# Gathering softmax row sums across partitions: one tile per parity, the first 32 partitions' sums left in place, three transfers in place of four

## The chip, the cores and the metric

The kernel runs on one core of a Trainium2 chip. The metric is device time in microseconds (us), the median of several runs. Beside the timed runs stands one profiled execution, from which every duration below is read.

## The reference, cut to what matters

Batch 8, 12 heads, 448 positions, head width 64. Attention comes first, with a soft cap on the scores, then a channel mix (RWKV style) over the 768 columns that the heads make together.

```python
scores = cap * tanh((q @ k.T) / sqrt(64) / cap)
attn = exp(scores - max);  attn = attn / (sum(attn, -1) + 1e-9)
x = attn @ v                                  # 8 x 448 x 768
xk, xr = mu_k * x + (1 - mu_k) * x_prev, mu_r * x + (1 - mu_r) * x_prev
v = relu(xk @ w_k) ** 2 @ w_v
out = sigmoid(xr @ w_r) * v
```

## The kernel before

Two heads make a pair, and 48 pairs are worked through in steps, one pair a step, followed by a few steps that only drain. The order of the work in a step is written out by hand as a string of operation names (`ROWS`, `ODD_6`, `LAST` and others), and each engine and each DMA queue executes its part of that string in order. After the steps (from about 529 us on) TensorE does the two large products with `w_v` and `w_r` and nothing else.

In a step for pair i, TensorE computes transposed scores in four groups of keys (`scores`), ScalarE applies tanh and exp, and VectorE sums the exponentials over keys. A score tile has keys on partitions, so this sum is split: `red` (line 347) transposes blocks of 32x32 and adds, which leaves on each of the four groups of 32 partitions one partial sum for every query. The sums of a pair stand in a tile `r1` of 128 partitions x 98 columns; there are two such tiles, for even and for odd i (shown in the trace as `r`).

What follows is a chain over two steps. In the string of step i+1, `gather` (line 353) issues four transfers on SP's queue, each of which moves one group of 32 partitions into a slot of `sq`, a tile of 32 partitions with eight slots, of which there is one for all pairs. `recip` (lines 357 to 364) adds the slots on VectorE, takes the reciprocal and transposes it. `rec_store` (line 367) writes it to memory from SP's queue, and `rec_load` (line 376) reads it back on SP's queue as a broadcast, two transfers into `r`. In step i+2 `norm` (line 380) multiplies the attention result in PSUM (`pv`) by it, `mix_old` (ScalarE) and `mix_new` (line 395, tile `xk`) blend it with the previous position, and that frees the PSUM bank for a later `pv`. From `xk` come the operands `xkh` and `xkl` of the product with `w_k` (line 472 and 496).

SP's queue carries nearly all other transfers too, in this order within a step of the middle of the kernel: `gather`, `weight_store` (w_d, line 614), `load_v` (rv, line 208), a weight load (line 544), `x_store` (line 424), `rec_store`, stores of k (line 521), `load_qk` (rqk, line 204) and `rec_load`. In the first six steps `rec_load` and `load_v` stand behind `gather`. Every transfer is bound to one of eight completion semaphores in turn, and is not issued before the transfer eight places ahead of it has completed.

Of the kernel before, what the change touches and what calls it, by code (L numbers as in the profile page):

```python
# [10 lines left out]
F32 = mybir.dt.float32  # L11
# [18 lines left out]
P = 128  # L30
# [17 lines left out]
NB = 2 * S // 32  # L48
RM = 3 * NB
RC = RM + NB // 2  # L50
# [57 lines left out]
class Body:  # L108
# [54 lines left out]
    def guard(self):  # L163
        nc = self.nc
        if self.maxima:
            nc.vector.memset(self.grd, 1e-9)
        else:
            nc.scalar.activation(self.grd, self.cap_t, AF.Abs)
            nc.scalar.activation(self.grd, self.grd, AF.Exp, scale=-1.0)
            nc.vector.tensor_scalar(self.grd, self.grd, 1e-9, None, op0=ALU.mult)  # L170
        nc.gpsimd.tensor_copy(self.sq[:, 6:8, RM:RC], self.grd[0:32].unsqueeze(2).to_broadcast([32, 2, NB // 2]))


    def init_x(self, pool):
# [6 lines left out]
    def init_sums(self, pool):  # L181


        nc = self.nc
        self.r1, self.sr = [], []
        self.sq = pool.tile([32, 8, RC], F32, name="sq_")
        for j in range(2):
            self.r1.append(pool.tile([P, RC], F32, name=f"r1_{j}"))
            self.sr.append(pool.tile([32, 32], F32, name=f"sr_{j}"))
            nc.gpsimd.memset(self.sr[j], 1.0)  # L190

# [157 lines left out]
                                     axis=mybir.AxisListType.X, op=ALU.add, apply_transpose=True)  # L349

    def gather(self, i):
        for q in range(4):
            self.nc.sync.dma_start(self.sq[:, q % 2 * 2 + q // 2], self.r1[i % 2][32 * q:32 * q + 32])  # L353

    def recip(self, i):
        nc, t, sq = self.nc, self.sr[i % 2], self.sq
        nc.vector.tensor_reduce(out=sq[:, 4:6, RM:RC], in_=sq[:, 0:4, 0:RM].rearrange("l q (h b g) -> l h b q g", h=2, g=3),
                                axis=mybir.AxisListType.XY, op=ALU.add)
        nc.vector.tensor_reduce(out=t[:, 0:NB].rearrange("l (h b) -> l h b", h=2),
                                in_=sq[:, :, RM:RC].rearrange("l (s h) b -> l h b s", h=2),  # L360
                                axis=mybir.AxisListType.X, op=ALU.add)
        nc.vector.reciprocal(t[:, 0:NB], t[:, 0:NB])
        self.rs[i] = self.up.tile([32, 32], F32, name="rs")
        nc.vector.transpose(out=self.rs[i], in_=t)
# [714 lines left out]
```

## Time and profile before

| | us |
|---|---|
| three timed runs | 899.71, 900.53, 900.52; median 900.52 |
| profiled execution, its own time | 896.04 |
| its span, from the first to the last instruction | 894.2 |
| TensorE busy | 860.9 (96%) |
| VectorE busy | 734.1 (82%) |

The profiled execution lies 4.48 us under the median, and 1.84 us of its time lie around its span. TensorE (PE in the profile, PEld its weight loads) is busy nearly throughout; the share says nothing yet on single stretches. DVE is VectorE, ACT ScalarE, POOL GpSimd, SPq SP's queue.

### The profile page before, as it was taken

The numbers are of one execution on the slowest core, as the hardware profiler recorded it, in microseconds if no ns is written. First come the engines' busy times: TensorE is split into PE (matmuls) and PEld (weight loads), VectorE is DVE, ScalarE is ACT, GpSimd is POOL, SyncE is SP. The second block draws the span as 40 slices with busy tenths as digits, with TensorE's granted clock in tenths as the row PEclk, the third lists the DMA queues.
The fourth block names the chain that finished last, engine by engine and source line by source line (L and its number), as shares of the span: only waits on it lengthen the run. The fifth ranks groups of instructions, "written<-read, shape, count | busy, mean of one in ns | idle before, by whom it ended". The sixth has DMA issues, their size and how long they took to land.

```text
span 894.2 us, 16687 instructions
## 1 busy us (share of the span) xinstructions
PE 860.9 (96%) x5826; PEld 705.7 (79%) x5826; DVE 734.1 (82%) x1246; ACT 625.2 (70%) x922; POOL 410.6 (46%) x345
## 2 busy tenths in 40 slices
PE   6789999999999999999999999999999999999996
PEld 2236667776766777777766799999999999999996
DVE  6989996999989989998978766887887757777775
ACT  8898888878888888788786564656565535555553
POOL 4996684777877867766853200000000033333330
PEclk9999999999999999999999999999999999999998
DMA  5565746566767667666665547554545546676763
GB/s 161 163 203 171 249 148 200 177 202 211 235 200 219 199 190 231 211 207 197 183 204 169 199 146 232 193 161 153 174 152 170 164 153 195 213 219 218 217 217 106
DMA packets 123679, 170.15 MB, mean 190 GB/s; under 512 B 22592, under 2 KB 107712, under 8 KB 123584
## 3 DMA queue, kind: packets, MB, share of 16 engines
q1 hardware_dynamic: 120848, 164.65, 59.0%
q10 hardware_dynamic: 2736, 4.33, 1.3%
q8 instruction: 48, 0.79, 0.4%
q14 instruction: 47, 0.39, 0.2%
HBM read 109.91 MB, written 56.60 MB: 186 GB/s over the span
## 4 chain that ended last, share of the span: by engine, by line
PE 72%; DVE 9%; DMA 6%; ACT 6%; POOL 3%; SPq 3%; issue 2%; ACTq 0%; DVEq 0%; POOLq 0%
PE ps L709 40%; PE kps L496 13%; PE pv L312 8%; PE s L275 5%; PE kps L472 3%; DVE r L347 3%; ACT p L288 2%; ACT p L301 2%; SPq L353 2%; DMA sq__195<-r 2%; PE pv L338 2%; PE s L268 1%; DMA rec_d<-rs 1%; DMA rv<-v 1%; DMA rqk<-qk 1%
## 5 line engine op out<-in xcount | busy, mean ns | idle before, releaser
L347 DVE TRANSPOSE_TENSOR_REDUCE r<-p 128x28 f32<-128x896 f32 (+1 forms) x192 | 181.1, 971 | 13.4 <-ACT p L301 13.4
L288 ACT ACTIVATE p<-s,scl_t 128x896 f32<-128x896 f32 x168 | 165.6, 998 | 26.8 <-PE s L268 22.5
L301 ACT ACTIVATE p<-p,cap_t 128x896 f32<-128x896 f32 x168 | 175.1, 1042 | 4.3 <-ACT ko L508 0.4
L673 POOL TENSOR_TENSOR s<-src 128x384 f32<-128x384 f32 x14 | 14.3, 1021 | 262.7 <-DVE lo L694 262.7
L312 PE MATMUL pv<-p,rv 128*64 128x448 f32 x576 | 119.8, 554 | 12.1 <-DVE xk L395 10.9
L709 PE MATMUL ps<-wvh,hi 128*128 128x384 f32 x392 | 131.1, 334 | 0.0
L709 PE MATMUL ps<-wvl,hi 128*128 128x384 f32 x392 | 131.0, 334 | 0.0
L693 ACT CAST hi<-s 128x512 fp32r<-128x512 f32 (+1 forms) x112 | 63.5, 567 | 89.6 <-PE ps L709 76.0
L694 DVE TENSOR_TENSOR lo<-s,hi 128x512 fp32r<-128x512 f32 (+1 forms) x112 | 70.8, 632 | 58.5 <-ACT hi L693 43.8
L132 POOL TENSOR_TENSOR qkl<-rqk,qkh 128x896 fp32r<-128x896 f32 x47 | 109.2, 2324 | 8.3 <-ACT qkh L126 4.8
L496 PE MATMUL kps<-xkh,wkh 64*128 64x448 f32 (+1 forms) x540 | 109.6, 367 | 0.0
L496 PE MATMUL kps<-xkl,wkh 64*128 64x448 f32 (+1 forms) x540 | 108.7, 362 | 0.0
L496 PE MATMUL kps<-xkh,wkl 64*128 64x448 f32 (+1 forms) x540 | 108.6, 361 | 0.0
L709 PE MATMUL ps<-wrh,hi 128*128 128x384 f32 x294 | 98.9, 336 | 0.3 <-DVE o L732 0.3
L709 PE MATMUL ps<-wrl,hi 128*128 128x384 f32 x294 | 98.8, 336 | 0.0
L312 PEld LDWEIGHTS pv<-p,rv 128*64 128x64 f32 x576 | 38.2, 138 | 76.5 <-issue 48.9
L693 ACT CAST hi<-src 128x512 fp32r<-128x512 f32 (+1 forms) x84 | 47.7, 568 | 62.0 <-PE ps L709 56.3
L709 PE MATMUL ps<-wvh,lo 128*128 128x384 f32 x392 | 83.7, 334 | 0.0
L694 DVE TENSOR_TENSOR lo<-src,hi 128x512 fp32r<-128x512 f32 (+1 forms) x84 | 57.3, 682 | 21.3 <-ACT hi L693 19.5
L709 PEld LDWEIGHTS ps<-wvh,hi 128*128 128x128 f32 x392 | 73.6, 188 | 0.3 <-issue 0.2
L709 PEld LDWEIGHTS ps<-wvl,hi 128*128 128x128 f32 x392 | 73.6, 188 | 0.0
L591 POOL TENSOR_TENSOR wsq<-wa,wsq 128x384 f32<-128x384 f32 (+1 forms) x40 | 43.9, 1096 | 62.9 <-DVE wsq L584 55.4
(118 smaller groups left out, 1915.0 us busy)
## 6 DMA issues: line engine op xcount, KB each, us to landing
rqk<-qk SPq DMA_DIRECT2D x47, 448.0 KB
src<-k_d SPq DMA_DIRECT2D x56, 256.0 KB
rv<-v SPq DMA_DIRECT2D x48, 256.0 KB
r<-rec_d SPq DMA_DIRECT2D x96, 112.0 KB
v_d<-o SPq DMA_DIRECT2D x56, 192.0 KB
src<-x_d SPq DMA_DIRECT2D x42, 256.0 KB
vl<-v_d SPq DMA_DIRECT2D x56, 192.0 KB
out<-o SPq DMA_DIRECT2D x55, 192.0 KB
```

Source lines behind the costliest of these rows:

```text
L132: {"p": self.nc.gpsimd, "v": self.nc.vector}[e].tensor_sub(*a)
L275: nc.tensor.matmul(s[:, (h + i) % 2, 0:S], qk[a][p, k], qk[b][p, 0:S], start=(n == 0), stop=(n == 2))
L288: self.nc.scalar.activation(p32[:, n], self.S.pop((i, g))[:, n, 0:S], AF.Tanh, scale=self.scl_t)
L301: self.nc.scalar.activation(p32, p32, AF.Exp, scale=1.0 if self.maxima else self.cap_t)
L312: nc.tensor.matmul(pv[p, 0:S], v[:, g, h, :], ph[:, (h + i) % 2, :], start=(g == 0), stop=False)
L347: self.nc.vector.tensor_reduce(out=r1[:, 0:RM].rearrange("p (x g) -> p x g", g=3)[:, :, g] if g < 3 else r1[:, RM:RC], in_=p32.rearrange(" ...
L472: nc.tensor.matmul(self.kps[fc][:, 0:S], w, m[:, dc, :], start=first, stop=last)
L496: self.nc.tensor.matmul(self.kps[c][:, 0:S], w[p, dc, c * P:(c + 1) * P], m[p, dc, :], start=s == 0, stop=last or way == 2 and t == 2, ski ...
L591: {"p": self.nc.gpsimd, "v": self.nc.vector}[e].tensor_add(sq, f(a), sq)
L693: self.nc.scalar.copy(hi, x)
L694: self.nc.vector.tensor_sub(lo, x, f(hi))
L709: self.nc.tensor.matmul(o, a[:, c, :], w[:, c, :], start=first and k == 0, stop=last and k == len(todo) - 1, skip_group_check=True)
```

## The change

The two tiles `r1` and the one tile `sq` become two tiles of 128 partitions x 8 slots x 98 columns, one for each parity. Slot 0 takes the partial sums of all 128 partitions, so those of the first 32 partitions are already where `sq` wants them. `gather` issues transfers for the other three groups only, out of slot 0 of the tile into slots 2, 1 and 3 of the same tile. `recip` reads the tile of its parity. The small constant in slots 6 and 7 is written once for each of the two tiles.

```diff
-        nc.gpsimd.tensor_copy(self.sq[:, 6:8, RM:RC], self.grd[0:32].unsqueeze(2).to_broadcast([32, 2, NB // 2]))
+        for sq in self.sq:
+            nc.gpsimd.tensor_copy(sq[:, 6:8, RM:RC], self.grd[0:32].unsqueeze(2).to_broadcast([32, 2, NB // 2]))
...
-        self.r1, self.sr = [], []
-        self.sq = pool.tile([32, 8, RC], F32, name="sq_")
+        self.r1, self.sr, self.sq = [], [], []
         for j in range(2):
-            self.r1.append(pool.tile([P, RC], F32, name=f"r1_{j}"))
+            t = pool.tile([P, 8, RC], F32, name=f"sq_{j}")
+            self.r1.append(t[:, 0])
+            self.sq.append(t[0:32])
...
     def gather(self, i):
-        for q in range(4):
-            self.nc.sync.dma_start(self.sq[:, q % 2 * 2 + q // 2], self.r1[i % 2][32 * q:32 * q + 32])
+        for q in range(1, 4):
+            self.nc.sync.dma_start(self.sq[i % 2][:, q % 2 * 2 + q // 2], self.r1[i % 2][32 * q:32 * q + 32])
 
     def recip(self, i):
-        nc, t, sq = self.nc, self.sr[i % 2], self.sq
+        nc, t, sq = self.nc, self.sr[i % 2], self.sq[i % 2]
```

Line numbers behind line 171 grow by up to two. On SP's queue the order of the other transfers stays, but with one transfer fewer in each step the semaphores are dealt out differently. Here is SP in a step of the middle (the one whose rv load is issued at 343 us), before; a name in `waits` that begins with DMAHW is one of the eight completion semaphores, and a transfer without such a wait is one whose semaphore was waited for already:

```order
L204 DMA rqk<-qk 128x896 [waits DMAHW0_49,PE_49]
L376 DMA r<-rec_d_97 64x448 [waits DMAHW5_49,DMAHW1_49]
L376 DMA r<-rec_d_97 64x448 [waits DMAHW2_49]
L353 DMA sq__195<-r_0_196 32x98 [waits DMAHW3_49,DVE_49]
L353 DMA sq__195<-r_0_196 32x98 [waits DMAHW4_49]
L353 DMA sq__195<-r_0_196 32x98
L353 DMA sq__195<-r_0_196 32x98 [waits DMAHW6_49]
L614 DMA w_d<-wsq 128x384 [waits DMAHW7_49,Pool_49]
L208 DMA rv<-v 128x512 [waits DMAHW0_49]
L544 DMA w_4387<-wv 128x768 [waits DMAHW1_49]
```

And the same step with the change:

```order
L206 DMA rqk<-qk 128x896 [waits DMAHW0_49,PE_49]
L378 DMA r<-rec_d_97 64x448 [waits DMAHW5_49,DMAHW1_49]
L378 DMA r<-rec_d_97 64x448 [waits DMAHW2_49]
L355 DMA sq_195<-sq_195 32x98 [waits DMAHW3_49,DVE_49]
L355 DMA sq_195<-sq_195 32x98 [waits DMAHW4_49]
L355 DMA sq_195<-sq_195 32x98
L616 DMA w_d<-wsq 128x384 [waits DMAHW6_49,Pool_49]
L210 DMA rv<-v 128x512 [waits DMAHW7_49]
L546 DMA w_4354<-wv 128x768 [waits DMAHW0_49]
```

One of the four transfers of 32x98 is gone; the transfer that waits for semaphore 0, on which the rqk load of the same step completes, was the rv load and is now the weight load behind it.

On VectorE nothing moves. Around the `recip` of pair 46, near the end of the steps, VectorE's rows are these before:

```order
L380 TENSOR_TENSOR x_163<-pv,r 128x448 [waits DMAHW7_49,DMAHW0_49,PE_49]
L357 TENSOR_REDUCE sq__195<-sq__195 32x2x14 [waits DMAHW3_49,DMAHW4_49,DMAHW2_49,DMAHW1_49]
L359 TENSOR_REDUCE sr_197<-sq__195 32x28 [waits DVE_49]
L362 RECIPROCAL sr_197<-sr_197 32x28 [waits DVE_49]
L364 STREAM_TRANSPOSE rs<-sr_197 32x32 [waits DVE_49]
L395 SCALAR_TENSOR_TENSOR xk<-x_163,mu_k,pv 128x448 [waits Activation_49]
```

and these with the change:

```order
L382 TENSOR_TENSOR x_163<-pv,r 128x448 [waits DMAHW2_49,DMAHW1_49,PE_49]
L359 TENSOR_REDUCE sq_195<-sq_195 32x2x14 [waits DMAHW4_49,DMAHW5_49,DMAHW3_49,DVE_49]
L361 TENSOR_REDUCE sr_196<-sq_195 32x28 [waits DVE_49]
L364 RECIPROCAL sr_196<-sr_196 32x28 [waits DVE_49]
L366 STREAM_TRANSPOSE rs<-sr_196 32x32 [waits DVE_49]
L397 SCALAR_TENSOR_TENSOR xk<-x_163,mu_k,pv 128x448 [waits Activation_49]
```

The first reduction waits for three transfers and for VectorE's own earlier sums, where it waited for four transfers.

## Rows read from the trace of the kernel before

**Rows 1.** The page, part 1: busy us, share of the span, instructions.

```profile
PE 860.9 (96%) x5826; PEld 705.7 (79%) x5826; DVE 734.1 (82%) x1246; ACT 625.2 (70%) x922; POOL 410.6 (46%) x345
```

**Rows 2.** Windows of 50 us: busy us of each engine, granted clock, DMA share, GB/s.

```profile
0.00:50.00 50.00, 34.67 (x192) 14.25 (x194) 38.68 (x74) 42.98 (x51) 36.36 (x39) 0.96 0.57 175
...
450.00:500.00 50.00, 47.84 (x354) 33.49 (x351) 39.37 (x55) 31.21 (x39) 21.43 (x18) 1.00 0.51 167
```

**Rows 3.** Waits of PE, 0 to 131 us: total us, times, longest.

```profile
PE pv L312 <- DVE xk L395: 9.3, 7, 3.0
```

**Rows 4.** Waits of PE, 131 to 440 us.

```profile
PE s L275 <- ACT turned L503: 1.3, 4, 0.3
PE pv L312 <- DMA rv<-v: 1.3, 3, 0.5
```

**Rows 5.** Waits of PE, 440 to 530 us.

```profile
PE kps L472 <- ACT ko L508: 1.6, 2, 1.1
PE pv L312 <- DVE xk L395: 1.6, 1, 1.6
```

**Rows 6.** Tile sq: engine, duration in ns (min/median/max), first and last start.

```profile
L353 SPq DMA_DIRECT2D sq__195<-r x192: 517/582/1572, 15.0 to 495.7; - x192
...
L171 POOL COPY sq__195<-grd x1: 197/197/197, 10.6 to 10.6; 32x28 f32<-32x28 f32 x1
```

**Rows 7.** Timeline of SP's queue, 338 to 345 us: start, us, line.

```profile
339.50 2.93 SPq L353 DMA_DIRECT2D sq__195<-r  x4
...
343.10 0.43 SPq L208 DMA_DIRECT2D rv<-v  x1
```

**Rows 8.** Chain of waits, 340 to 346 us: start, us, what.

```profile
343.10 3.77 DMA rv<-v
```

**Rows 9.** Chain of waits, 440 to 470 us: one round of the sums.

```profile
453.56 0.54 SPq L353
...
455.41 1.79 DMA sq__195<-r
...
458.81 3.71 DMA rec_d<-rs
...
463.76 0.54 SPq L353
```

**Rows 10.** Chain of waits, 485 to 503 us.

```profile
487.30 1.79 DMA sq__195<-r
...
490.67 0.56 DVE xk L395
...
495.67 3.17 DMA sq__195<-r
...
500.25 0.61 DVE x L380
```

**Rows 11.** Waits of DVE, whole span: total us, times, longest.

```profile
DVE sq__195 L357 <- DMA sq__195<-r: 14.0, 19, 1.9
```

**Rows 12.** Waits of SP's queue, whole span.

```profile
SPq L376 <- DMA rec_d<-rs: 69.6, 42, 5.0
```

**Rows 13.** Timeline of POOL, 5 to 36 us; in brackets idle time before.

```profile
18.15 1.01 POOL L591 TENSOR_TENSOR wsq<-wa,wsq 128x384 f32<-128x384 f32 x1 [4.30 <-DVE wsq L584]
...
35.06 1.00 POOL L591 TENSOR_TENSOR wsq<-wa,wsq 128x384 f32<-128x384 f32 x1 [0.25 <-DVE wsq L584]
```

**Rows 14.** Timeline of SP's queue, 10 to 64 us.

```profile
22.05 0.36 SPq L204 DMA_DIRECT2D rqk<-qk  x1
22.52 2.42 SPq L353 DMA_DIRECT2D sq__195<-r  x4
```

**Rows 15.** Timeline of DVE, 10 to 64 us.

```profile
27.83 0.51 DVE L357 TENSOR_REDUCE sq__195<-sq__195 32x28 f32<-32x336 f32 x1 [1.00 <-DMA sq__195<-r]
```

**Rows 16.** Timeline of DVE, 500 to 535 us: the last operands prepared for w_v.

```profile
516.16 3.56 DVE L835 TENSOR_TENSOR wvl<-wvl,wvh 128x768 fp32r<-128x768 f32 x4
```

**Rows 17.** Tile wvh, 500 to 560 us: the first weight load of the last stage.

```profile
L709 PEld LDWEIGHTS ps<-wvh,hi x60: 187/188/188, 529.1 to 559.3; 128*128 128x128 f32 x60
```

## The prediction

> **What bounds the kernel now.** The page's first part comes first: TensorE is busy for 860.9 of 894.2 us [rows 1], so no change to transfers can be worth more than some 33 us, and the question is where those lie. The windows of 50 us tell [rows 2]. In the first, TensorE is busy for only 34.67 us; at the end of the steps it is idle for 2.16 us in 50. Behind 529 us it does nothing but matmuls, and what those need is ready early: the last operand for `w_v` is made at 516.16 + 3.56 = 519.7 us and the first weight load of that stage starts at 529.1 [rows 16, 17]. So whatever brings TensorE earlier to the end of the steps comes off the end of the span, as long as it stays under that lead of 9 us.
>
> Next I asked what TensorE waits for, stage by stage. Up to 131 us its largest wait is for `xk`, 9.3 us [rows 3]; from there to 440 us it waits for 2.6 us in all, half of that for the load of rv [rows 4]; from 440 us to the end of the steps it waits for 3.2 us, for a PSUM bank freed by `xk` and for k sums taken over by ScalarE [rows 5]. A gain must come out of these three sums. The chain of waits then shows why the transfers of the sums matter at all: near the end of the steps it runs round and round through them [rows 9, 10].
>
> **What the change removes.** One issue on SP's queue in each of 48 steps. An issue takes 0.58 us in the median [rows 6]; four took 2.42 us and 2.93 us at the two places shown [rows 7, 14], and from the first issue at 453.56 to the last at 455.41 are 1.85 us, three spacings of 0.62 [rows 9]. After the last issue begins, the data are there 1.79 us later [rows 9, 10]. I take **0.61 us**: the last group starts so much earlier, and everything behind it on SP (w_d, rv, the weight load, `x_store`) too.
>
> The semaphores may help as well: in the step shown the rv load stands eight places behind the rqk load of 448 KB and waits for it, and with the change the weight load stands there. TensorE shows no rv wait longer than 0.5 us [rows 4], which the 0.61 cover already, so I add nothing for it. Behind the weight load on SP stand `x_store` and `rec_store`; it reaches that wait at the very time at which rv reached it before, so they lose nothing either.
>
> **What it adds.** One more copy of 0.20 us on POOL at 10.6 us [rows 6]; POOL then stands idle for 4.30 us before its work at 18.15 [rows 13], which covers it; uncovered it would cost 0.2 us once. The reduction on VectorE now also waits for VectorE's own earlier sums. The transfers for which it waits read those same sums, so the sums are always done first: nothing. The sums, the reductions and the reciprocal keep their shapes.
>
> **First stage, 0 to 131 us.** Here VectorE, ScalarE and POOL share the limit. At 27.83 the reduction waited 1.00 us for the gather [rows 15], but right ahead of that gather stands an rqk load of 448 KB [rows 14]: the last of the four issues ended at 24.94 and the data landed 2.9 us later, where 1.79 less the issue, 1.2 us, is usual. The landing may thus be that of rqk. What follows is caught by POOL, which waited for VectorE only 0.25 us at 35.06 [rows 13]. Term: 0.2 us; bounds 0 and 0.6 (one issue, if the landing counts in full).
>
> **Middle, 131 to 440 us.** Three times TensorE stands still for rv, together 1.3 us, none longer than 0.5 us [rows 4]. In the chain at one of them, rv is issued at 343.10 directly behind the four gathers and the w_d store and lands 3.77 us later, just ahead of the matmul that waited [rows 7, 8]. Issued 0.61 us earlier, all three waits vanish. Term: 1.3 us; bounds 0.4, if so much of the 3.77 us is traffic ahead of rv that only a quarter of the lead, 0.15 us, arrives each time, and 1.3, since no more is waited.
>
> **End of the steps, 440 to 505 us.** One round from the first gather to the next is 463.76 - 453.56 = 10.2 us [rows 9]: 1.85 of issues, 1.79 to land, 1.6 on VectorE, 3.71 until the stored reciprocal is back, and `rec_load` with 1.25 ahead of the next gather. With 0.61 off each round this circle has slack against TensorE. What remains is the drain. The gather of pair 46 is tied to its sums and ends 0.61 us earlier; `xk` at 490.67 follows, and the wait of 1.6 us for it shrinks to 1.0 [rows 5, 10]. The gather of pair 47 stands behind the `rec_load` of pair 46, so it gains that 0.61 and its own, 1.2 in all; `norm` at 500.25 follows it [rows 10], then the k sums, whose longest wait was 1.1. TensorE by then is 0.6 ahead, so that wait falls by 0.6. That is 1.2. If the rounds ahead also give their slack to ScalarE, the first of the two k waits (1.6 - 1.1 = 0.5) goes too: 1.7 to 1.8. Term: **1.8 us**; bounds 0.6 (one issue only, the landing of 3.17 us at 495.67 being other traffic) and 3.2 (all of [rows 5]).
>
> Sum: 0.2 + 1.3 + 1.8 = **3.3 us**, with bounds 1.0 and 0.6 + 1.3 + 3.2 = 5.1. Of the profiled 896.04 us that leaves 892.7; the median of the runs lies 4.48 us higher, and 900.52 - 3.3 = 897.2.
>
> A sentence of the Trainium skill speaks against this: "DMA: Bandwidth & Descriptors", section "Issuing engines are not separate DMA queues", calls the time that a sequencer takes to start a DMA usually small relative to the DMA itself; by that rule the removed issue would be hidden beside the other three and the sum would be about zero. The trace does not agree for these small transfers, 0.58 us of issue against 1.79 until landing, and the first rival is what the rule would do here.
>
> **Rivals.**
>
> *Hidden.* Four small transfers overlap, and what counts is when the queue gets to them. For it: the landing of 3.17 us at 495.67 against 1.79 [rows 10], and that at 27.83. VectorE waited for these data only 19 times out of 48, 14.0 us in all [rows 11]; in the other 29 steps they were early anyway. Against it: two of the three gather landings of [rows 9, 10] are at 1.79, so nothing stands ahead of them. It gives the lower bounds, 1.0 us, or a little less where SP's lead is lost again behind a later wait: about 0.8 us, 899.7 us.
>
> *Slower.* The stored reciprocal comes back later. SP waited for it 42 times, 69.6 us, so 1.66 in the mean, but up to 5.0 [rows 12]: it depends on which large load is in flight. Loads that start 0.61 us earlier can move into its way between 440 and 490 us, where the chain of waits runs through it round by round [rows 9]. Two waits of that stretch at 5.0 in place of the mean would cost 6.7, less the 3.3: 903.9 us. It decides from 1.7 us more in each of two rounds. Against it: the loads and the reciprocal move together by the same 0.61.
>
> *Larger.* The circle of the sums, not TensorE, sets the pace from 440 us on, and all idle time there goes, and the other terms come at their upper bounds: 5.1 us, 895.4 us.
>
> **How the numbers follow.** A measurement of this kernel can tell about 0.2%, 1.8 us, from no change. Chances: forecast 0.60 (its own range 895.4 to 898.7), hidden 0.27, slower 0.09, larger 0.04. Faster by over 0.2% are forecast and larger, 0.64; within 0.2% is hidden, 0.27; slower 0.09. The range runs from 895.0, just past the upper bound, to 900.6, which takes in most of hidden; slower and the edges stay out.
>
> **What would show it.** In the trace after: 144 transfers at the gather's line in place of 192, groups of three with 1.8 us of issues; no wait of TensorE for rv between 131 and 440 us; the VectorE wait for sq well under 14.0 us (some 19 x 0.6 less, so 3 to 6); TensorE's waits from 440 us on at 1.4 us rather than 3.2; the first weight load of the last stage at about 525.8 in place of 529.1. The first stage should end within half a us of before. If the gather's landings grow by as much as the issue that was dropped, hidden is right; if SP's wait at line 378 grows beyond 70 us, slower is. The prediction would be wrong altogether if TensorE's own pace changed somewhere, which nothing in the diff touches.

## The result, and the profile after

After the change the kernel takes **891.31 us** (median of 4 executions, 890.04 to 892.17) against 900.52 before: ratio 0.9896, 95% interval 0.9878 to 0.9914. That is 9.2 us less, where 3.3 were forecast, and below the range. The profiled execution of the kernel after took 892.08 us.

The kernel after, the page's part 1 (compare [rows 1]) and the shares of the chain that ended last:

```profile
PE 863.4 (97%) x5826; PEld 707.2 (79%) x5826; DVE 731.0 (82%) x1246; ACT 626.7 (70%) x922; POOL 410.6 (46%) x346
...
PE 76%; DVE 11%; ACT 5%; DMA 4%; issue 2%; SPq 1%; POOL 0%; ACTq 0%; DVEq 0%; POOLq 0%
```

The kernel after, all that TensorE waits for from 131 to 440 us (compare [rows 4]); from 440 to 530 us the same view is empty (compare [rows 5]):

```profile
PE s L277 <- ACT turned L505: 1.3, 4, 0.3
```

The kernel after, tile sq (compare [rows 6]), then waits of VectorE (compare [rows 11]), and of SP's queue (compare [rows 12]; columns: total us, times, longest):

```profile
L355 SPq DMA_DIRECT2D sq<-sq x144: 517/582/1786, 14.8 to 490.3; - x144
```

```profile
DVE sq L359 <- DMA sq<-sq: 2.5, 4, 1.0
```

```profile
SPq L369 <- DVE rs L366: 81.6, 43, 4.6
...
SPq L378 <- DMA rec_d<-rs: 39.7, 31, 5.0
```

An issue less is in the trace, the rv waits of TensorE are gone, and so is every wait from 440 us on. The first weight load of the last stage (compare [rows 17]):

```profile
L711 PEld LDWEIGHTS ps<-wvh,hi x392: 186/188/188, 524.2 to 727.1; 128*128 128x128 f32 x196
```

Where the time went is read best in one stretch with the same work in both kernels: from the store of the reciprocal of pair 20 (of 0 to 47) to the first weight load of the last stage. Here are the windows of that stretch: its bounds, its length, TensorE's busy time and matmuls, then the busy time of its weight loads, of VectorE, ScalarE and POOL, the granted clock, the DMA share and GB/s. First the kernel before, in the execution that was profiled ahead of the prediction, then in a second one (run b_copy), then the kernel after and a second execution of that (run a_copy):

```profile
223.67:529.10 305.43, 299.82 (x2369) 221.33 (x2366) 267.62 (x429) 238.95 (x312) 191.28 (x153) 1.00 0.64 202
```

```profile
226.38:532.80 306.42, 300.30 (x2369) 221.36 (x2366) 267.01 (x429) 238.92 (x312) 191.66 (x153) 1.00 0.64 202
```

```profile
224.27:524.20 299.93, 298.90 (x2370) 221.42 (x2367) 264.82 (x429) 239.21 (x312) 191.90 (x153) 1.00 0.64 203
```

```profile
223.28:523.00 299.72, 298.73 (x2370) 221.65 (x2367) 264.74 (x429) 238.67 (x312) 191.69 (x153) 1.00 0.63 203
```

The same matmuls take 305.4 and 306.4 us before, 299.9 and 299.7 after: **5.5 to 6.7 us** of the gain lie here. TensorE's idle time (length less busy) falls from 5.6 and 6.1 us to 1.0. The rest, 0.9 to 1.6 us, is busy time. Most of it is in the `pv` matmuls of L312 (L314 after), the ones that had waited: 66.1 and 66.5 us before, 65.0 and 65.1 after. That they are counted as busy while held up is likely, but not shown.

Where in the stretch TensorE gains can be read from the same eight matmuls near 430 us, in the same four executions, in the same order:

```profile
431.97 0.98 PE L338 MATMUL pv<-p,rv 64*64 64x448 f32 x8
```

```profile
434.63 0.98 PE L338 MATMUL pv<-p,rv 64*64 64x448 f32 x8
```

```profile
430.61 0.98 PE L340 MATMUL pv<-p,rv 64*64 64x448 f32 x8
```

```profile
429.34 0.98 PE L340 MATMUL pv<-p,rv 64*64 64x448 f32 x8
```

From the start of the stretch to them are 208.3 us before and 206.3 and 206.1 after, 2.0 to 2.2 us less; from them to the last stage 97.1 and 98.2 before and 93.6 and 93.7 after, 3.5 to 4.5 less.

The pace shows on SP's timeline at the store of the reciprocal, pair 20 and pair 47, 27 rounds apart. Before, after, and with five transfers (run e3, below):

```profile
223.67 0.34 SPq L367 DMA_DIRECT2D rec_d<-rs  x1
...
500.34 0.33 SPq L367 DMA_DIRECT2D rec_d<-rs  x1
```

```profile
224.27 0.34 SPq L369 DMA_DIRECT2D rec_d<-rs  x1
...
494.10 0.33 SPq L369 DMA_DIRECT2D rec_d<-rs  x1
```

```profile
229.95 0.34 SPq L368 DMA_DIRECT2D rec_d<-rs  x1
...
525.70 0.33 SPq L368 DMA_DIRECT2D rec_d<-rs  x1
```

A round is 276.67 / 27 = 10.25 us before, 9.99 after and 10.95 with five. The table below gives this mean round for the other kernels.

### The profile page after: what moved, and what is told of

The parts are those of the page before. It is cut to its first block, busy times and chain, and to the rows that moved or that the text cites. A ratio compares the mean times of both kernels' runs of the same rounds, so it can differ in the third digit from the quotient of the medians.

```text
span 890.3 us, 16622 instructions
## 1 busy us (share of the span) xinstructions
PE 863.4 (97%) x5826; PEld 707.2 (79%) x5826; DVE 731.0 (82%) x1246; ACT 626.7 (70%) x922; POOL 410.6 (46%) x346
## 4 chain that ended last, share of the span: by engine, by line
PE 76%; DVE 11%; ACT 5%; DMA 4%; issue 2%; SPq 1%; POOL 0%; ACTq 0%; DVEq 0%; POOLq 0%
PE ps L711 40%; PE kps L498 14%; PE pv L314 8%; PE s L277 6%; PE kps L474 4%; DVE sq L349 4%; ACT p L290 2%; ACT p L303 2%; DMA sq<-sq 2%; PE pv L340 2%; PE s L270 1%; DMA rqk<-qk 1%; DVE wa L580 1%; DVE xk L397 1%; PE s L474 1%
## 5 line engine op out<-in xcount | busy, mean ns | idle before, releaser
L349 DVE TRANSPOSE_TENSOR_REDUCE sq<-p 128x28 f32<-128x896 f32 (+1 forms) x192 | 181.6, 972 | 17.1 <-ACT p L303 17.1
L314 PE MATMUL pv<-p,rv 128*64 128x448 f32 x576 | 120.6, 560 | 8.8 <-DVE xk L397 8.7
L314 PEld LDWEIGHTS pv<-p,rv 128*64 128x64 f32 x576 | 38.4, 139 | 72.5 <-issue 48.6
```

The lines of the kernel that those rows point to most:

```text
L314: nc.tensor.matmul(pv[p, 0:S], v[:, g, h, :], ph[:, (h + i) % 2, :], start=(g == 0), stop=False)
L349: self.nc.vector.tensor_reduce(out=r1[:, 0:RM].rearrange("p (x g) -> p x g", g=3)[:, :, g] if g < 3 else r1[:, RM:RC], in_=p32.rearrange(" ...
```

## The experiments

Each was timed beside the kernel before on the same chip, 5 to 12 executions each (10 of b_copy).

| run | median us | ratio to before [95%] | mean round us |
|---|---|---|---|
| b_copy | 898.93 | 0.9979 [0.9961, 0.9997] | 10.28 |
| a_copy | 890.69 | 0.9896 [0.9861, 0.9932] | 9.99 |
| e1_four_issues | 898.54 | 0.9985 [0.9966, 1.0003] | 10.24 |
| e2_two_tiles | 900.38 | 0.9994 [0.9973, 1.0016] | 10.35 |
| e3_five_issues | 924.39 | 1.0261 [1.0235, 1.0287] | 10.95 |
| e6_copy | 893.31 | 0.9921 [0.9891, 0.9950] | 10.00 |
| e4_before_reload_late | 910.55 | 1.0120 [1.0098, 1.0143] | 10.62 |
| e5_after_reload_late | 893.62 | 0.9935 [0.9916, 0.9954] | 10.13 |
| e7_one_reload | 965.77 | 1.0741 [1.0718, 1.0764] | |
| e8_after_one_reload | 952.08 | 1.0589 [1.0565, 1.0613] | |
| e9_fourth_last | 898.57 | 0.9980 [0.9959, 1.0001] | 10.16 |
| e10_fifth_behind_store | 904.96 | 1.0046 [1.0023, 1.0069] | 10.52 |
| f1_fourth_last_store_first | 891.59 | 0.9898 [0.9875, 0.9922] | 10.00 |
| f2_before_store_first | 892.48 | 0.9911 [0.9889, 0.9934] | 10.07 |
| f3_after_store_first | 889.86 | 0.9878 [0.9854, 0.9902] | 10.05 |
| g1_five_store_first | 901.63 | 1.0014 [0.9997, 1.0030] | 10.21 |

The rounds of the f runs and of g1 are not quite comparable with the others: they move the store of pair 20 ahead and leave that of pair 47 where it was. Counted to pair 46 instead (26 rounds), after, a_copy, e6, f1, f2 and f3 are alike at 10.07 to 10.08 us, the kernel before is at 10.27 and g1 at 10.23.

**The two kernels again.**

> The kernel before, unchanged, for a second profile. Its profiled execution so far (896.04 us) lies 4.5 us under its timed median (900.52 us). If that execution was an unusually quick one, a second profile reads 899 to 902 us, and the extra 4 us show as idle time of TensorE between 440 and 530 us (more than the 3.2 us of the first profile), with the synchronization engine's rounds there longer than 10.2 us. If the profiler itself makes the kernel quicker, it reads 895 to 897 us again, with the same waits. The timed median is 900 to 901 us in either case.

> The kernel after, unchanged, for more executions of it. Its four executions so far spread over 2.1 us (890.04 to 892.17), while those of the kernel before spread over 6.6 us (897.5 to 904.1). If in the kernel before the round lets every late landing through to the end, and in the kernel after the slack of the round takes it up, the spread stays at 2 to 4 us and the median at 890.5 to 892. If the four were only lucky: a spread of 6 us.

The profile of b_copy is of an execution of 900.25 us, so the first one, 896.04, lay at the low end of what this kernel does, and being profiled did not by itself make it so. But its extra 4 us are not where the expectation put them: the stretch above is only 1.0 us longer. In the first 172 us it is 2.7 us later (the store of pair 15 at 174.93 against 172.19), with a mean granted clock of 0.93 up to 131 us where the first profile had 0.97; e6_copy read 0.93 there too. A copy of the kernel before measured 0.2% below it, with an interval that leaves out 1; so far can two medians lie apart for no reason. The kernel after stayed between 890.0 and 893.3 us in 10 executions; that of before went from 895.65 to 907.16 over all runs, some hundred executions.

**The issue or the tile?**

> The kernel after, with a fourth transfer of a 32-partition piece put first in each group, into 84 columns of the sums' tile that nothing reads. The theory of the round (an issue less in the synchronization engine's round of gather, wait for the reciprocal's store, reload is what the change gains): the gain goes, 898 to 901 us, and the rows of the reciprocal's store come back to the times of the kernel before from pair 40 on. The rival theory of the tile (two tiles by parity, and the first piece needing no transfer, are what gains): it stays at 890 to 893 us, since both of these are left as they are after the change.

```diff
 def gather(self, i):
+    self.nc.sync.dma_start(self.sq[i % 2][:, 6, 0:RM], self.r1[i % 2][0:32, 0:RM])
     for q in range(1, 4):
```

> The kernel before with the gathered rows in two places by parity (partitions 0 to 31 and 32 to 63 of one tile), all four transfers kept and the partial sums in their own tiles. The theory of the round: nothing gained, 899 to 902 us. The theory of the tile: most of the gain, 891 to 894 us.

```diff
...
-        self.sq = pool.tile([32, 8, RC], F32, name="sq_")
+        u = pool.tile([64, 8, RC], F32, name="sq_")
+        self.sq = [u[0:32], u[32:64]]
...
```

> The kernel before with a fifth transfer in each group, into columns that nothing reads. The theory of the round: each issue more costs what the one dropped gave back, or more, since the round is past the pace of TensorE from its first step on: 0.6 us in each of the 13 to 24 rounds behind 230 us, so 908 to 915 us. The rival that the transfers are hidden, and that something else made the gain: 899 to 902 us.

```diff
 def gather(self, i):
+    self.nc.sync.dma_start(self.sq[:, 6, 0:RM], self.r1[i % 2][0:32, 0:RM])
     for q in range(4):
```

> The kernel before with its one tile for the gathered rows, in which the first of the four transfers is replaced by a copy on VectorE of the same 32 partitions: an issue less, and neither the second tile nor the sums in place. The theory of the round: nearly the whole gain, less about 0.2 us in a round for the copy, 890 to 894 us. The theory of the tile: 899 to 902 us.

```diff
-        for q in range(4):
+        self.nc.vector.tensor_copy(self.sq[:, 0], self.r1[i % 2][0:32])
+        for q in range(1, 4):
```

All four go the way of the round. With four transfers and everything else of the change, the gain is all but gone (898.5, within the noise of the kernel before). Two places for the rows by themselves (with the reciprocal's tiles laid out in the same way) gain nothing (900.4). An issue less without the tiles of the change gives most of it: 893.3, and 10.00 us a round. The stretch from pair 20's store to the last stage shows it too, in e1_four_issues as long as before, in e6_copy as long as after:

```profile
224.06:529.30 305.24, 300.32 (x2370) 221.82 (x2367) 267.33 (x429) 238.92 (x312) 191.70 (x153) 1.00 0.65 202
```

```profile
226.82:526.70 299.88, 298.80 (x2369) 221.65 (x2366) 270.19 (x456) 238.78 (x312) 192.08 (x153) 1.00 0.64 203
```

The fifth costs 23 us, more than was expected: I had counted the rounds behind 230 us, but in that run they fall behind from pair 16 on (its store is at 185.35 us, in the kernel after at 182.32, while pair 15's are at 173.38 and 172.72), and then by 0.7 us a round against the kernel before.

**Through which leg?** The first attempts to break the round both went wrong.

> The kernel before with four transfers, but from the step of pair 23 on the reload of the stored reciprocals stands behind the next step's gather instead of ahead of it; the number of issues stays. If the round (gather, reciprocal, store, its landing, reload, next gather) is what makes each issue count, the gather no longer waits for the landing, and the time falls to about that of the kernel after, 889 to 895 us, and TensorE has no idle time from 440 to 530 us. The rival, that it is the mere number of issues on the synchronization engine's queue that counts: 899 to 902 us, as before.

> The kernel after with the same move of the reload. The theory of the round: there is nothing more to win, since TensorE has no wait left from 440 to 530 us, 889 to 892 us; it loses only if the reload now comes too late for VectorE's multiplication. If the round still costs something in an ordinary execution of the kernel after: 886 to 889 us.

```diff
-ROWS = """gather weight_store load_v quad_load quad_load weight_load 135:U 3:turn PE 135:red3 f f f f f tanh0 exp0 0:turn 0:PE_TURN red0
+ROWS = """gather rec_load weight_store load_v quad_load quad_load weight_load 135:U 3:turn PE 135:red3 f f f f f tanh0 exp0 0:turn 0:PE_TURN red0
...
-15:exp2 red2 weight_rest weight_sum 0:relu 024:exp3 024:red3 weight_abs load_qk rec_load PE_END"""
+15:exp2 red2 weight_rest weight_sum 0:relu 024:exp3 024:red3 weight_abs load_qk PE_END"""
```

(The same exchange stands in `LAST`. `ROWS`, and so this edit and the later exchange in it, holds from pair 13's store on: the first reload that moves is that of pair 13, not of pair 23 as the expectation says.) Four transfers ahead of the reload made it 10 us slower; both theories missed that. The chain of waits of e4_before_reload_late shows why:

```profile
449.77 0.58 SPq L353
450.39 0.59 SPq L353
451.02 0.60 SPq L376
451.67 2.86 DMA r<-rec_d
```

The reload now stands behind the four issues and, with its landing, in the round, because VectorE's multiplication (L380) waits for it and the next reciprocal stands behind that multiplication on VectorE. Its wait there rose from 6.6 us in 10 times to 38.3 in 36. The round was not broken, only led another way. With three transfers the same move costs 2 to 3 us (893.6).

> The kernel before, its four transfers left, with the two transfers of the reload merged into one for the even pairs: half an issue fewer per round, and none of the change's tiles. The theory of the round: any issue in it counts alike, so near half of the change's gain of 9.2 us, 894 to 898 us. The theory of the tile, and that of the gather's place in VectorE's wait: 899 to 902 us.

> The kernel after with the same merged reload. The theory of the round: the round is already shorter than TensorE's step, so nothing more, 889 to 892 us. If each issue costs its time wherever it stands, it gains as much again as in the kernel before, 885 to 888 us.

```diff
+        if i % 2:
+            for h in range(2):
...
+        else:
+            self.nc.sync.dma_start(r, self.rec_d[i].unsqueeze(1).to_broadcast([2, 64, S]))
```

(For even pairs one transfer takes the place of the two of the half rows.) Both missed by 50 us and more, and they tell nothing of issues: the merged transfer is far slower. In e7_one_reload, SP's timeline, then VectorE's, then the chain:

```profile
445.07 0.56 SPq L379 DMA_DIRECT2D r<-rec_d  x1
```

```profile
452.96 0.62 DVE L383 TENSOR_TENSOR x<-pv,r 128x448 f32<-128x448 f32 x1 [3.53 <-DMA r<-rec_d]
```

```profile
447.57 6.06 DMA sq__195<-r
```

From the end of its issue (445.63) until VectorE could use it 7.3 us pass, and the gather behind it lands after 6.06 us where 1.8 is usual [rows 9]. The two transfers of the kernel before, on the same timelines, took 455.85 - (452.34 + 1.12) = 2.4 us from the end of their issue:

```profile
452.34 1.12 SPq L376 DMA_DIRECT2D r<-rec_d  x2
```

```profile
455.85 0.63 DVE L380 TENSOR_TENSOR x<-pv,r 128x448 f32<-128x448 f32 x1 [0.69 <-DMA r<-rec_d]
```

> The kernel after with the same unread fourth transfer as before, but put behind the three others, so that VectorE's reciprocal doesn't wait for it. If an issue costs because it stands between the reload and the last piece that the reciprocal needs: no cost, 890 to 893 us. If any issue on the synchronization engine's queue costs: 898 to 900 us, as with the fourth transfer first.

```diff
         for q in range(1, 4):
             ...
+        self.nc.sync.dma_start(self.sq[i % 2][:, 6, 0:RM], self.r1[i % 2][0:32, 0:RM])
```

> The kernel before with a fifth, unread transfer issued right behind the store of the reciprocals, where the queue would next wait for the landing of that store; the fifth ahead of the other four took 924 us. If only what lengthens the round costs: 899 to 903 us. If the number of issues costs: 922 to 926 us.

```diff
     def rec_store(self, i):
         ...
+        self.nc.sync.dma_start(self.sq[:, 6, 0:RM], self.r1[i % 2][0:32, 0:RM])
```

In e9 VectorE's reciprocal waits for the three real transfers alone, and still nearly the whole gain is gone (the stretch is 304.2 us long): that expectation fell. In e10 the fifth costs 5 us, not 23 as ahead of the gather: so the number of issues doesn't decide either, but that place isn't free. Why e9 costs can be read from SP's timeline of e9_fourth_last, one round:

```profile
452.81 1.12 SPq L379 DMA_DIRECT2D r<-rec_d  x2
454.02 1.81 SPq L355 DMA_DIRECT2D sq<-sq  x3
455.88 0.59 SPq L356 DMA_DIRECT2D sq<-sq  x1
456.51 0.58 SPq L210 DMA_DIRECT2D rv<-v  x1
457.14 0.43 SPq L815 DMA_DIRECT2D w<-w_d  x1
457.62 0.48 SPq L815 DMA_DIRECT2D wsq<-w_d  x1
458.21 0.39 SPq L427 DMA_DIRECT2D x_d<-xg  x1
458.71 0.36 SPq L370 DMA_DIRECT2D rec_d<-rs  x1
459.47 0.85 SPq L524 DMA_DIRECT2D k_d<-ko  x2
463.33 1.12 SPq L379 DMA_DIRECT2D r<-rec_d  x2
```

From the reload to the store the queue issues without a pause, 458.71 - 452.81 = 5.9 us, and then, but for two stores of k, it stands for the landing until 463.33. The queue is a leg of its own, and any issue from the reload to the store lengthens it. In the kernel after the same leg has a gap ahead of the store, where SP waits for the reciprocal: 0.7 us in the corresponding round (pair 43), 1.6 us in the next one, which is shown here and is the usual size (median of pairs 21 to 46; 0.1 in e9):

```profile
459.93 1.39 SPq L378 DMA_DIRECT2D r<-rec_d  x2
461.41 1.81 SPq L355 DMA_DIRECT2D sq<-sq  x3
463.27 0.58 SPq L210 DMA_DIRECT2D rv<-v  x1
463.89 0.95 SPq L814 DMA_DIRECT2D w<-w_d  x2
465.15 0.33 SPq L426 DMA_DIRECT2D x_d<-xg  x1
467.05 0.33 SPq L369 DMA_DIRECT2D rec_d<-rs  x1
```

So the next runs left the number of issues alone and moved one of them out of that leg.

> The kernel after with the unread fourth transfer behind the three others, and with the reciprocal's store issued ahead of the step's store of x (an issue of 0.4 us, in one step in six two more) instead of behind it, from pair 14 on. If the queue's leg from the reload to that store is what the fourth transfer lengthened, most of its cost goes: 891 to 895 us. If any issue counts wherever it stands: 898 to 900 us, since none is taken away.

> The kernel before with the same exchange: the reciprocal's store ahead of the store of x. All four transfers stay ahead of the reciprocal, so the leg through VectorE (reload, four issues, landing, reciprocal) is as long as it was. If that leg is about as long as the queue's, little is gained: 896 to 900 us. If the queue's leg alone sets the round: 891 to 895 us. If any issue counts wherever it stands: 899 to 902 us.

> The kernel after with the same exchange. TensorE has no idle time left behind 131 us but 1.3 us, so nothing is to be had from a shorter round: 890 to 892 us by every theory of the round; below 889 us would mean that the round still costs time in it.

```diff
-weight_sum tanh1 15:PE_TURN exp1 23:relu red1 gate_new norm recip x_store 1:k_put rec_store 235:k_put qk_high qk_low 024:tanh3 tanh2 0234:exp2 4:turn mix_old mix_new x_high x_low gate_old
+weight_sum tanh1 15:PE_TURN exp1 23:relu red1 gate_new norm recip rec_store x_store 1:k_put 235:k_put qk_high qk_low 024:tanh3 tanh2 0234:exp2 4:turn mix_old mix_new x_high x_low gate_old
```

f1 wins all of it back (891.6), with as many issues as e9. f2 is the kernel before with two neighbours on SP exchanged, and it has nearly the whole gain of the change (892.5). It takes 0.4 us of issue out of the queue's leg, in every sixth round 0.9 more, where the change takes 0.6 in each, and none out of the leg through VectorE; so it seems to give more than the issue. f3, 889.9 us, is the lowest of all kernels; its interval overlaps that of the kernel after.

> The kernel before with five transfers in the gather (alone 924 us) and the reciprocal's store ahead of the store of x. The exchange takes an issue of 0.4 us out of the queue's leg, and it also puts the small store ahead of 224 KB in its queue, so that it may land earlier. If only the issue matters, the fifth issue (0.6 us) is not made good by it, and the time is near or above that of the kernel before, 903 to 915 us. If the earlier landing matters too, by some 1.3 us a round, the fifth issue is paid for: 890 to 898 us.

(The edit is that of e3 and f2 together.) The result, 901.6, lies between the two expectations and 23 us below e3. The issues that the exchange takes out of the leg are 0.4 us in some 34 steps and 0.9 more in every sixth, 14 + 5 = 19 us if all of it counted, less than the 23; that points to the landing. Waits of SP's queue for the stored reciprocal, 230 to 500 us, in e3_five_issues and in g1_five_store_first:

```profile
SPq L377 <- DMA rec_d<-rs: 44.1, 24, 3.9
```

```profile
SPq L377 <- DMA rec_d<-rs: 11.5, 11, 1.7
```

The landing is seen to be earlier. Placed ahead of the 224 KB of `x_store`, the 3.5 KB of the reciprocal let SP go on sooner: from the start of the store to the start of the reload on SP's timeline the median over these rounds is 2.31 us against 3.12 (2.30 in f2 against 3.16 before). The kernels without the exchange fit this. From the start of the store of x to the reload pass 4.4 us in the kernel before, 4.3 in e1 and 4.3 in e9 (medians of pairs 21 to 46), although the reciprocal's store stands 1.3, 1.4 and 1.1 us behind that of x; so in e9, where the reciprocal is stored sooner, the reload comes hardly sooner. In the kernel after it stands 1.9 us behind, and 1.9 us later comes the reload. How the gain divides between the issue and the landing these runs don't tell.

## Why the prediction was wrong in size

- **What bounds.** Right: the gain had to come out of TensorE's waits, and the last stage starts earlier by what is saved (524.2 us; 525.8 forecast). Its length differs by 1.0 us at most: from its first weight load to the end of the span are 365.1 and 365.7 us before, 366.1 and 365.9 after.
- **Cost of an issue, 0.61 us.** Right as a duration: 0.58 us in the median, 144 transfers, groups of three 1.81 us. The forecast of VectorE's wait for sq, 3 to 6 us, came to 2.5.
- **First stage, 0.2 us.** Not shown: the store of pair 11 is at 133.42 us against 132.89, 0.5 us later, and one execution differs there from the next by more than that (b_copy 135.38, a_copy 132.21). More on this below.
- **Middle, 1.3 us.** Too small. The three waits for rv are gone as forecast. But SP's rounds were held up here too: from pair 20's store to pair 40's they take 205.3 us before (428.97 - 223.67) and 202.0 after (426.28 - 224.27). TensorE itself gained 2.0 to 2.2 us up to its eight matmuls near 430 us, past the upper bound of 1.3 ("no more is waited"); I took a queue that falls behind to cost no more than the waits beside it.
- **End of the steps, 1.8 us: the step that failed.** I held the drain of the last two pairs to be all that remains, and left 1.4 us of [rows 5] standing. All of it went, and the held-up busy time too: 3.5 to 4.5 us behind the eight matmuls, past the upper bound of 3.2. With 10.2 us a round I had the round in hand [rows 9], but wrote only that it "has slack against TensorE" with 0.61 off; I didn't ask how much TensorE had been waiting for it all along. The measured size of the middle and the end together is 5.5 to 6.7 us, where I had 3.1.
- **The rivals.** "Larger", at 0.04, had the mechanism: the circle of the sums, not TensorE, sets the pace. Even it stopped at 5.1 us, since it counted the listed waits of one execution alone. "Hidden" is refuted by e1, e6 and the empty view of TensorE's waits; "slower" by SP's wait at the reload, 39.7 us and not above 70. The Trainium skill's remark that the time to start a DMA is usually small beside the DMA ("DMA: Bandwidth & Descriptors", "Issuing engines are not separate DMA queues") does not hold for these small transfers: 0.58 us of issue stand against 1.79 until the data are there [rows 6, 9], and 5.9 us of a round of 10.5 us in e9 are issues.
- **The base.** The sum was made against an execution of 896.04 us that lay near the low end of what the kernel before does. It showed less waiting than b_copy does, by 0.5 us in the stretch. Against this execution 892.7 was forecast, and the profiled execution after took 892.08; that is luck. The stretch gave 5.5 us there, and 1.6 were lost again around it, 0.6 ahead of it and 1.0 in the last stage.

**Still open** is where the other 2.5 to 3.7 us of the 9.2 lie. In a pair of profiles, b_copy against a_copy, the difference ahead of the stretch is 226.38 - 223.28 = 3.1 us, all of it in the first 172 us; the first profiles, 223.67 and 224.27, show none there. Neither kernel's first stage is the same from one execution to the next.

The other profiles make it likely that the change shortens this stage after all, and not by the issue. The first stage of the kernel before was profiled four times (before, b_copy, e4, f2; the edits of e4 and f2 act later): the store of pair 11 lies at 132.9, 135.4, 138.0 and 133.1 us. That of the kernel after was profiled four times too (after, a_copy, e5, f3): 133.4, 132.2, 131.7 and 133.2. The means are 134.8 and 132.6. Three kernels with the sums left in place and four issues (e1, e9, f1) are at 132.8 to 133.3, like the kernel after; five without the sums in place (e2, e3, e6, e10, g1) at 134.3 to 136.7. So some 2 us may belong to the sums left in place. The medians of runs timed together go the same way: e6 is 2.6 us above a_copy, though its copy on VectorE may have a part in that, and f2 2.6 above f3. But each profile is a single execution, the two groups overlap, and the reason stays open. The mean granted clock up to 131 us was 0.95 to 0.96 in the seven profiles with the sums in place and 0.92 to 0.97 in the nine others.

What is shown: the 5.5 to 6.7 us of the stretch are the issue in the round and not the tiles (e1, e2, e6); it counts by its place and not by the number of issues (e9 against f1, e3 against g1, e10); and a leg of the round runs through SP's queue up to the store and its landing. That the way through VectorE's reciprocal is a second leg of nearly the same length is argued, not shown: from 230 to 500 us SP does wait 18.1 us in 21 rounds for the reciprocal in the kernel before, but e9, which shortens that way, is only 1 to 2 us shorter in the stretch than the kernel before, and f2, which leaves four issues in it, has nearly the whole gain (the earlier landing shortens that way too).

## What to carry to other kernels

Where a chain goes through a store, its landing and a reload on one queue, compare its round with the step of the engine that should set the pace: a queue that was within 3% of it cost more here than the waits listed for that engine in one execution, and a fraction of a microsecond per round adds up over the rounds. Look at what stands on the queue between the reload and the store, and at what stands ahead of the small store: an exchange of two neighbouring operations gave here nearly what the change gave. Before merging transfers, look at how long the merged one takes to land.

## What the runs showed of the hardware

- One transfer into 128 partitions, written as two rows each repeated 64 times, held VectorE's multiplication until 7.3 us after its issue, and the transfers behind it on the queue 6.06 us. In the kernel before, where two transfers of 64 partitions take its place, VectorE began 2.4 us after the issue ended. The Trainium skill ("DMA: Bandwidth & Descriptors", "Rules for kernel authors") says that an outermost dimension smaller than 16, such as a leading broadcast, confines a transfer to at most that many engines. The long landing of this one, whose outermost dimension is 2, agrees with it; which engines worked was not looked at.
- The time that a store of 3.5 KB holds its queue hung on its neighbour: from store to reload passed 3.0 to 3.2 us when it was issued 1.3 to 1.4 us behind one of 224 KB (before, b_copy), 1.9 when 1.9 us behind it (after), and 2.3 when ahead of it (f2, g1; the issue of the large store is in these 2.3).
